# A Fourier mixing layer and an ELU feed-forward block: the first tile's opening, reordered

## The chip, the core and the metric

The kernel runs on one core of a Trainium2 chip. A core has five engines with instruction streams of their own: TensorE (PE, matrix products; its loads of stationary operands are listed as PEld), VectorE (DVE), ScalarE (ACT), GpSimd (POOL) and SyncE (SP, which here only issues transfers). Sixteen DMA engines carry what SP and POOL issue. The metric is device time in microseconds (us) of one launch.

## The reference

```python
def _attn_ref(x, filt_r, filt_i):            # x: 8 x 3008 x 256, filters: 1505 x 256
    X = np.fft.rfft(x, axis=1)
    F = (filt_r + 1j * filt_i)[None, :, :]
    Y = X * F
    return np.fft.irfft(Y, n=x.shape[1], axis=1).astype(np.float32)

def _moe_ref(x, w_in, w_out):                # x: 24064 x 256, w_in: 256 x 2048, w_out: 2048 x 256
    h = x @ w_in
    g = np.where(h > 0.0, h, np.exp(np.minimum(h, 0.0)) - 1.0)
    return (g @ w_out).astype(np.float32)
```

The second function takes the result of the first, its 8 batches of 3008 rows put one after the other. x and the filters are float32 at the kernel, and the weights arrive as float64.

## The kernel before, in words

The DFT of length 3008 is split as 47 x 64. The forward transform has a first factor of length 64 (`a_...`, tables `tf`, `ta`), and a second of length 47 (`b_...`, tables `gf`, later `fb`); then come the products with the filter; the inverse goes back by a 47-factor (`bi_...`) and a 64-factor (`n_...`). The feed-forward block follows tile by tile: an item is (batch, one of 6 row tiles, one of 4 quarters of d_ff), and both of its matrix products are done with seven block products in place of eight (`up_steps`, `down_steps`, with `w_sums` and `n_sums` forming the sums of blocks). Batch b + 1 is transformed beside the feed-forward block of batch b. The order of all instructions is the order in which the program writes them: each engine runs its own in that order. A dictionary `plan` puts the transform's and the conversion's pieces at five places inside each item (0 to 4).

The opening is the transform of batch 0, where no feed-forward work can lie beside it. Its parts:

- `x_place_first`, `x_load_first` (L256 to L277): 24 pairs of rows in six chunks. SP issues two transfers of x per chunk and one of the tables `tf` (for chunks 2 and 3, 4 and 5 one transfer for both). A chunk's 64 x 64 table of cosines and sines is stored twice, in the halves of the table's columns that serve the two parts of the spectrum, with other signs.
- `a_first` (L279): eight matmuls per chunk into PSUM, four ScalarE copies into `zt` (which partly lies in the room of `w_in[3]` and `w_out[3]`). `t_first` (L294) transposes it for a group of frequencies.
- `f_read_first` (L323): the filter, in four parts (two halves of the frequencies, `gh`, by two halves of the rows, `a`); half 0 of the rows by SP, half 1 by POOL.
- the loop over eight groups: `b_first` (L360, forward matmuls into two PSUM tiles, then `products`, four VectorE operations, L351 to L354), inside it `bi_first` of two groups earlier (L368: inverse matmuls, and two ScalarE copies, L380 and L381, into one of two halves of `t3f`, for the last two groups of `t2`), then `t_first` of two groups later and `y_write_first` (L386, four SP transfers to DRAM). The halves of `t3f` are used in turn, so the copies of group g wait for the write of group g - 2.
- `y_read_first` (L396) reads the first four rows of each part back as `t4f`, for `n_first`, which makes the first row tile; then the first item's matmuls begin.

The 16 weight blocks k (four per quarter: two of `w_in`, two of `w_out`) are brought from float64 to float32 by `w_fetch` (transfer, L740), `w_split` (two VectorE masks on the upper word, L769 and L770), `w_float` (four ScalarE steps: lower word, mantissa, two for the exponent, L779), `w_join` (VectorE: sign, lower word added, product, L785 to L798) and, after each odd k, `w_sums` (four additions, L806 to L809). `WTMP` says which of four sets of temporary tiles block k uses. In the kernel before, blocks 0 to 3 are fetched by SP between the chunks of x and converted there, 4 to 8 fetched by POOL after the filter and converted beside the loop (`BESIDE`) and after it, 9 to 15 inside the first six items (`early`).

Of the kernel before, what the change touches and what calls it, by code (L numbers as in the profile page):

```python
# [11 lines left out]
FP32 = mybir.dt.float32  # L12
# [26 lines left out]
SUMS = 4  # L39
WTMP = (0, 1, 2, 1, 0, 1, 0, 1, 0, 3, 2, 3, 2, 3, 2, 3)  # L40
# [4 lines left out]
def _make_tables():  # L45
# [30 lines left out]
    tf = np.ascontiguousarray(ta.reshape(P, H, 4, K2).transpose(0, 1, 3, 2)).reshape(P, H, P)  # L76
# [62 lines left out]
def kernel(  # L139
# [47 lines left out]
    edges = glob.tile([P, 3], FP32, name="edges")  # L187
# [66 lines left out]
    def x_place_first(c):  # L254
# [4 lines left out]
        if c < 2:  # L259
            w = tnp.tile([P, 4, P], FP32, tag="tn", name="tn")  # L260
        else:
            if c % 2 == 0:
                tas["pair", c // 2] = t4p.tile([P, 4, D], FP32, tag="t4", name="t0").rearrange("p u (w f) -> p (u w) f", f=P)
            w = tas["pair", c // 2][:, 4 * (c % 2):4 * (c % 2) + 4, :]
        xs[0, c], tas[0, c] = t, w
# [3 lines left out]
    def x_load_first(c):  # L269
# [4 lines left out]
        if c < 2:  # L274
            nc.sync.dma_start(tas[0, c], tf_d[:, 4 * c:4 * c + 4, :])
        elif c % 2 == 0:
            nc.sync.dma_start(tas.pop(("pair", c // 2)), tf_d[:, 4 * c:4 * c + 8, :])  # L277

    def a_first(c):  # L279
        xt, w = xs.pop((0, c)), tas.pop((0, c))  # L280
        for dh in range(2):
            k, ps = bank("psa", (P, 64, XC, 2))
            for u in range(XC):
                nc.tensor.matmul(ps[:, :, u, :], xt[:, u, ts(dh, P)], w[:, u, :].rearrange("p (k q) -> p k q", q=2),
                                 start=True, stop=True)
            for kh in range(2):
# [3 lines left out]
                s = ps[:, 32 * kh:32 * kh + 32].rearrange("p (k a) u q -> p k a (u q)", a=2)  # L290
                nc.scalar.activation(out=o, in_=s, func=AXT.Copy)
            banks.append(k)
# [30 lines left out]
    def f_read_first(gh, a, queue):  # L323

        r = slice(64 * a, 64 * a + 48)
        w0 = 1 if gh == a == 0 else 0
        k = 16 * a + 8 * gh
        for c, src in enumerate((filt_r, filt_i)):
            t = ff[r, c, 4 * gh:4 * gh + 4].rearrange("p g u d -> p (g u) d")
            queue.dma_start(t[0:48:2], raw(src, k, [[64 * D, 24], [D, 8], [1, D]]))  # L330
            for j, n in ((0, 16), (16, 7)):
                queue.dma_start(t[1 + 2 * j:2 * (j + n):2, w0:8],
                                raw(src, 64 * (j + 1) - k - w0, [[64 * D, n], [-D, 8 - w0], [1, D]]))
# [53 lines left out]
    def y_write_first(g, queues):  # L387
        if g == 0:
            yds[0] = yd.tile([P, H, D], FP32, tag="yd", name="yd")
        t = t3s.pop((0, g))  # L390
        for p in range(4):
            r = 64 * (p // 2) + 24 * (p % 2)
            k = 16 * g + 4 * p
            queues[p // 2].dma_start(yds[0][k:k + 4].rearrange("u i d -> i u d"), t[r:r + 24])
# [367 lines left out]
    def w_tmp(k):  # L762
        m, e, c = wtmp[WTMP[k]]
        return m, e, c[:, 0], c[:, 1]
# [7 lines left out]
    def w_float(k, *parts):  # L772
        m, e, f, l = w_tmp(k)
# [3 lines left out]
        for i in parts or range(4):  # L777
# [3 lines left out]
    def w_join(k):  # L781
        q, j = divmod(k, 4)
        m, e, f, l = w_tmp(k)
        hi = wds.pop(k)[:, :, 1]
        nc.vector.scalar_tensor_tensor(out=e, in0=hi, scalar=0x80000000, in1=e,  # L785
                                       op0=ALU.bitwise_and, op1=ALU.bitwise_or)
        nc.vector.tensor_tensor(out=f, in0=f, in1=l, op=ALU.add)
        e = e.bitcast(FP32)
        if j < 2:
            f, e = (t.rearrange("p (a j c) -> p a j c", a=2, j=2) for t in (f, e))  # L790
            dst = w_in[q][:, 2 * j:2 * j + 2, :, :].rearrange("p j a c -> p a j c")
# [300 lines left out]
```

## Time and profile before

| | us |
|---|---|
| median of 3 runs (2579.84 to 2589.81) | 2580.27 |
| profiled execution | 2585.88 |
| its span, first to last instruction | 2584.1 |
| TensorE busy (98% of the span) | 2526.8 |
| VectorE busy (80%) | 2070.1 |
| ScalarE busy (59%) | 1536.9 |
| GpSimd busy (7%) | 177.0 |

Busy times overlap, since the engines run beside each other. A row of an engine's timeline gives start, duration, engine, line, operation, output <- inputs with partitions x elements, and in brackets the idle time before it with what ended it. A row of waits gives the waiting engine and line, what it waited for, total us, number of times and the longest. Stretches are given in us from the start of the span. Releasers are inferred from semaphores and can be wrong where several were waited for.

### The profile page before, as it was taken

To read this page: it belongs to the slowest core of one execution; us is meant where nothing else is said; L and a number is where in the kernel's file an instruction comes from. 1 tells how busy PE (TensorE), PEld (TensorE's weight loads), DVE (VectorE), ACT (ScalarE), POOL (GpSimd) and SP (SyncE) were. 2 spreads that over 40 slices of the span, in tenths; PEclk is the share of its full clock that TensorE was granted. 3 is DMA by queue.
4 is the path that set the end of the run, shared out by engine and by line. 5 is a ranking of instruction groups with operands and counts; after the bars stand their busy time and mean duration, and the time that the engine had idled before them with its cause. 6 is when DMAs were issued, how large, how long until landed. Compare 5 with 4: busy or idle time off the path is not lost.

```text
span 2584.1 us, 44148 instructions
## 1 busy us (share of the span) xinstructions
PE 2526.8 (98%) x16726; PEld 2163.6 (84%) x16726; DVE 2070.1 (80%) x3613; ACT 1536.9 (59%) x2714; POOL 177.0 (7%) x308
## 2 busy tenths in 40 slices
PE   6789999999999999999999999999999999999998
PEld 4578888888898888988889888898888888898887
DVE  5889887788877888788887888778887788876766
ACT  5665556656566655665556655566556656565554
POOL 3130000001000100000000000000010001000000
PEclk8999999999999999999999999999999999999999
DMA  8652313522134222432215331253223322120010
GB/s 218 201 154 55 76 36 76 131 70 68 33 85 127 68 65 43 106 100 67 67 40 131 77 78 43 61 133 77 63 48 77 78 71 68 34 47 18 19 28 17
DMA packets 228994, 197.23 MB, mean 76 GB/s; under 512 B 128852, under 2 KB 202294, under 8 KB 228590
## 3 DMA queue, kind: packets, MB, share of 16 engines
q1 hardware_dynamic: 215550, 167.95, 26.7%
q0 software_dynamic: 12080, 26.21, 3.8%
q8 instruction: 132, 2.16, 0.4%
q14 instruction: 80, 0.66, 0.1%
q10 hardware_dynamic: 1152, 0.26, 0.1%
HBM read 122.46 MB, written 74.97 MB: 76 GB/s over the span
## 4 chain that ended last, share of the span: by engine, by line
PE 89%; DVE 6%; DMA 2%; ACT 2%; issue 1%; SPq 0%; POOL 0%; DVEq 0%; ACTq 0%; POOLq 0%
PE po L667 41%; PE phs L584 23%; PE phd L584 12%; PE pha L584 6%; PE pse L512 2%; PE psa L241 1%; PE pf L411 1%; PE pv L477 1%; DVE g L606 1%; DVE g L592 1%; ACT e L602 1%; PE po L345 0%; ACT e L601 0%; DVE g L643 0%; DVE g L642 0%
## 5 line engine op out<-in xcount | busy, mean ns | idle before, releaser
L667 PE MATMUL po<-g,wo 128*128 128x256 f32 (+1 forms) x5376 | 1317.3, 377 | 0.6 <-DVE t L686 0.6
L667 PEld LDWEIGHTS po<-g,wo 128*128 128x128 f32 x5376 | 1015.4, 191 | 164.8 <-issue 49.7
L595 ACT ACTIVATE g<-phs 128x512 f32<-128x512 f32 (+1 forms) x576 | 338.6, 588 | 713.8 <-PE phs L584 712.7
L584 PE MATMUL phs<-y,wi 128*128 128x256 f32 (+1 forms) x2288 | 582.4, 377 | 10.3 <-ACT g L595 10.3
L602 ACT ACTIVATE e<-e 128x512 f32<-128x512 f32 (+1 forms) x768 | 477.2, 621 | 24.3
L584 PEld LDWEIGHTS phs<-y,wi 128*128 128x128 f32 x2288 | 431.6, 191 | 65.3 <-ACT g L595 13.1
L592 DVE TENSOR_TENSOR g<-phd,g 128x512 f32<-128x512 f32 (+1 forms) x384 | 259.2, 675 | 267.4 <-ACT e L602 194.7
L606 DVE SCALAR_TENSOR_TENSOR g<-e,g 128x512 f32<-128x512 f32 (+1 forms) x576 | 390.6, 678 | 0.9 <-ACT e L602 0.5
L601 ACT ACTIVATE e<-g 128x512 f32<-128x512 f32 (+1 forms) x576 | 353.5, 614 | 60.0 <-DVE g L592 51.2
L606 DVE SCALAR_TENSOR_TENSOR g<-e,phs 128x512 f32<-128x512 f32 (+1 forms) x192 | 129.9, 676 | 141.0 <-ACT e L602 141.0
L584 PE MATMUL phs<-ys,wi 128*128 128x256 f32 (+1 forms) x784 | 198.6, 376 | 2.9 <-ACT g L595 2.9
L584 PE MATMUL phd<-y,wi 128*128 128x256 f32 (+1 forms) x768 | 194.9, 376 | 5.2 <-DVE g L592 5.2
L584 PE MATMUL phd<-ys,wi 128*128 128x256 f32 (+1 forms) x768 | 194.4, 376 | 1.2 <-DVE g L592 1.2
L584 PE MATMUL pha<-ys,wi 128*128 128x256 f32 (+1 forms) x752 | 190.1, 375 | 0.0
L601 ACT ACTIVATE e<-phs 128x512 f32<-128x512 f32 (+1 forms) x192 | 113.4, 591 | 111.7 <-PE phs L584 111.7
L584 PEld LDWEIGHTS phd<-y,wi 128*128 128x128 f32 x768 | 145.2, 190 | 25.0 <-DVE g L592 9.2
L584 PEld LDWEIGHTS phs<-ys,wi 128*128 128x128 f32 x784 | 147.9, 190 | 20.7 <-ACT g L595 4.2
L584 PEld LDWEIGHTS phd<-ys,wi 128*128 128x128 f32 x768 | 146.6, 191 | 17.8 <-DVE g L592 1.4
L340 POOL DMA_DIRECT2D fall<-fp x224 | 110.3, 500 | 691.6 <-DVE r L450 689.0
L584 PEld LDWEIGHTS pha<-ys,wi 128*128 128x128 f32 x752 | 143.1, 190 | 16.3
L592 DVE TENSOR_TENSOR g<-pha,g 128x512 f32<-128x512 f32 (+1 forms) x192 | 129.3, 673 | 24.3 <-PE pha L584 24.3
L643 DVE TENSOR_TENSOR g<-g,g 128x512 f32<-128x512 f32 (+1 forms) x192 | 132.6, 691 | 6.7
(181 smaller groups left out, 2167.8 us busy)
## 6 DMA issues: line engine op xcount, KB each, us to landing
t<-yd SPq DMA_DIRECT2D x94, 256.0 KB
z<-t SPq DMA_DIRECT2D x84, 256.0 KB
fall<-fp POOLq DMA_DIRECT2D x224, 96.0 KB, 2.9
t<-z SPq DMA_DIRECT2D x224, 96.0 KB
yd<-t SPq DMA_DIRECT2D x112, 192.0 KB
out_dram<-o SPq DMA_DIRECT2D x632, 32.0 KB
xc<-in_x_dram SPq DMA_DIRECT2D x84, 128.0 KB
xc<-in_x_dram SPq DMA_DIRECT2D x161, 64.0 KB
```

The costliest lines, as they stand in the source:

```text
L241: nc.tensor.matmul(p[o:o + 64, u, :], w[r, u, o:o + 64], src[r, u, :], start=True, stop=True)
L340: nc.gpsimd.dma_start(t[32 * a:32 * a + 24].rearrange("p c u d -> p (c u d)"), fp[g, a].rearrange("q c u d -> q (c u d)"))
L411: nc.tensor.matmul(pf[p][1][32 * a:32 * a + 32, js, :], fb[r, v, :], t2[r, js, a, :], start=True, stop=True, tile_position=(32 * p, 32 * a))
L512: nc.tensor.matmul(p[o:o + 64, dh, ds(64 * q, n)], t[r, i - 4 * m, ds(dh * P + o, 64)], w[r, i - 4 * m, 0:n], start=True, stop=True)
L584: nc.tensor.matmul(ps[:, a, 0:h], w_in[q][:, COMBO[n], a, :], y[n], start=start and a == 0, stop=True, skip_group_check=True)
L592: nc.vector.tensor_tensor(out=g[o], in0=i0, in1=i1, op=ALU.add)
L595: nc.scalar.activation(out=g[o], in_=i0, func=AXT.Copy)
L601: nc.scalar.activation(out=e, in_=src, func=AXT.Relu, scale=-1.0)
L602: nc.scalar.activation(out=e, in_=e, func=AXT.Exp, scale=-1.0)
L606: nc.vector.scalar_tensor_tensor(out=g[n], in0=es[n], scalar=1.0, in1=src, op0=ALU.subtract, op1=ALU.max)
L643: nc.vector.tensor_tensor(out=b12, in0=b22, in1=b12, op=ALU.subtract)
L667: nc.tensor.matmul(po[i][:, u, 0:h], w_out[q][:, COMBO[n], a, :], g[n][:, a, :], start=begin and a == 0 and n in (1, 3, 6, 4), stop=True, ...
```

## The change

Tables. `tf` holds only the first of the two copies; `ta_first` (new) writes the second with two VectorE multiplications per loaded table by a column of +1 and -1 (`edges[:, 3]`). `a_first` takes both PSUM banks of a chunk before its copies, and reads the table in the new layout.

Order of transfers. SP: x 0 and 1, weight 0, x 2 and 3, weight 1, x 4 and 5, `once`, two thirds of `gs`, then the filter in three portions (groups 0 and 1, 2 and 3, 4 to 7) with weight 2 after the second, then weights 3 and 4. POOL: the other halves of the three portions, weights 5 and 8, and 6 and 7 inside the loop. `t8` moves into the loop. The last two groups write four rows first, read them back, and write the other twenty after that. Weight 14 moves from the list before the items into the first item.

Conversion. `w_float` has three steps; the lower word is added in `w_join` by one multiply-add in place of an addition. Only block 0 is converted (and 1 split) before the loop, 1 to 3 beside it, 4 to 6 after it, 7 to 15 in the items; the sums of blocks 1, 3, 5 and 7 go from VectorE to POOL, those of 13 from POOL to VectorE. Three matmuls on a zeroed tile stand at the start.

```diff
-    tf = np.ascontiguousarray(ta.reshape(P, H, 4, K2).transpose(0, 1, 3, 2)).reshape(P, H, P)
+    tf = np.ascontiguousarray(ta.reshape(P, H, 4, 2, 16)[:, :, 0::2].transpose(0, 1, 3, 2, 4)).reshape(P, H, 64)
...
-        if c < 2:
-            nc.sync.dma_start(tas[0, c], tf_d[:, 4 * c:4 * c + 4, :])
-        elif c % 2 == 0:
-            nc.sync.dma_start(tas.pop(("pair", c // 2)), tf_d[:, 4 * c:4 * c + 8, :])
+        if ("load", c) in tas:
+            w, i, n = tas["load", c]
+            nc.sync.dma_start(w[:, 0], tf_d[:, i:i + n, :])
+
+    def ta_first(c):
+
+        w, _, _ = tas.pop(("load", c))
+        for a in range(2):
+            i, o = (w[:, q].rearrange("p u (h a k) -> p u h a k", h=2, a=2)[:, :, :, k] for q, k in ((0, a), (1, 1 - a)))
+            nc.vector.tensor_scalar(out=o, in0=i, scalar1=edges[:, 3:4], scalar2=None, op0=ALU.mult)
...
-    def y_write_first(g, queues):
+    def y_write_first(g, i0=0, i1=24):
...
-            queues[p // 2].dma_start(yds[0][k:k + 4].rearrange("u i d -> i u d"), t[r:r + 24])
+            nc.sync.dma_start(yds[0][k:k + 4, i0:i1].rearrange("u i d -> i u d"), t[r + i0:r + i1])
...
-        steps = ((l, wds[k][:, :, 0], AXT.Identity, 2.0 ** -52, 0.0), (f, m, AXT.Identity, 2.0 ** -20, 1.0),
+        steps = ((f, m, AXT.Identity, 2.0 ** -20, 1.0),
                  (ef, e, AXT.Relu, -8.0, edges[:, 0:1]), (e, ef, AXT.Relu, -1.0, edges[:, 1:2]))
...
-        nc.vector.tensor_tensor(out=f, in0=f, in1=l, op=ALU.add)
+                nc.vector.scalar_tensor_tensor(out=f, in0=lo, scalar=2.0 ** -52, in1=f, op0=ALU.mult, op1=ALU.add)
...
+            f_read_first(0, 2, 0, nc.sync)
+            f_read_first(0, 2, 1, nc.gpsimd)
+            f_read_first(2, 4, 0, nc.sync)
+            w_fetch(2, nc.sync)
+            f_read_first(2, 4, 1, nc.gpsimd)
+            f_read_first(4, 8, 0, nc.sync)
+            f_read_first(4, 8, 1, nc.gpsimd)
+            ta_first(0)
+            ta_first(1)
+            w_split(0)
+            ta_first(2)
+            ta_first(4)
+            for c in range(NXC):
+                a_first(c)
+                if c == 2:
+                    w_float(0)
+            w_join(0)
+            w_split(1)
+            for k in (3, 4):
+                w_fetch(k, nc.sync)
+            w_fetch(5)
...
+            w_fetch(8)
...
+            BESIDE = {0: ((w_float, 1, 0),), 1: ((w_split, 2), (w_float, 1, 1, 2)), 2: ((w_float, 2, 0), (w_join, 1, 0)),
+                      3: ((w_join, 1, 1), (w_float, 2, 1, 2)), 4: ((w_join, 1, 2), (w_sums, 1, nc.gpsimd), (w_fetch, 6), (w_split, 3)),
+                      5: ((w_join, 2, 0), (w_float, 3, 0)), 6: ((w_join, 2, 1), (w_float, 3, 1, 2)),
+                      7: ((w_join, 2, 2), (w_fetch, 7)), 8: ((w_join, 3), (w_split, 4))}
...
-                if g >= 2:
-                    y_write_first(g - 2, (nc.sync, nc.sync))
+                if 2 <= g < NG:
+                    y_write_first(g - 2)
+                elif g >= NG:
+                    y_write_first(g - 2, 0, 4)
+                if g == 4:
+                    nc.sync.dma_start(t8, t8_d)
                 if g == NG:
-                    y_read_first(0, 5)
-            y_read_first(5, 8)
+                    y_read_first(0, 6)
+            y_read_first(6, 8)
+            for g in (6, 7):
+                y_write_first(g, 4, 24)
+            w_sums(3, nc.gpsimd)
+            w_float(4)
+            w_split(5)
+            w_join(4)
+            w_float(5)
+            w_split(6)
+            w_join(5)
+            w_float(6)
+            w_sums(5, nc.gpsimd)
             w_split(7)
             w_join(6)
             w_float(7)
-            w_split(8)
-            w_sums(5)
-            w_float(8)
-            w_join(7)
-            w_sums(7)
-            w_join(8)
...
+        early = ((0, 2, w_join, 7, 0, 1), (0, 2, w_split, 8), (0, 4, w_float, 8, 0), (0, 0, w_float, 8, 1, 2), (0, 0, w_join, 7, 2),
+                 (0, 0, w_sums, 7, nc.gpsimd), (0, 3, n_unit, 0, 1), (0, 1, w_join, 8, 0, 1), (0, 1, w_split, 9), (0, 1, w_fetch, 14, nc.sync),
...
```

More of the change, by code (lines that the diff above doesn't have):

```diff
@@ L871 @@
-            step(0)
-            a_first(0)
-            step(1)
-            w_fetch(3, nc.sync)
-            x_load_first(5)
-            nc.sync.dma_start(once, once_d)
-            nc.sync.dma_start(gs, gs_d)
-            a_first(1)
-            f_read_first(0, 0, nc.sync)
-            f_read_first(0, 1, nc.gpsimd)
-            a_first(2)
-            step(2)
-            a_first(3)
-            step(3)
-            f_read_first(1, 0, nc.sync)
-            f_read_first(1, 1, nc.gpsimd)
-            w_fetch(4)
@@ L941 @@
             x_load(1, c)
-        for k in (11, 12, 13, 14, 15):
+        for k in (11, 12, 13, 15):
             w_fetch(k, nc.sync)
```

147 lines of the change are left out of this document (71 added, 76 removed).

## The prediction

> **What bounds it now.** I read the busy time by stretches first, cut where the kernel's stages begin, then the waits, then the engines' orders in time. The columns below are PE, PEld, DVE, ACT and POOL busy (instructions), granted clock, DMA share and GB/s.
>
> ```profile
> 0.00:9.00 9.00, 0.00 (x0) 0.03 (x1) 3.54 (x5) 1.95 (x2) 8.17 (x10) 1.00 0.78 190
> 9.00:25.40 16.40, 12.04 (x64) 11.70 (x65) 6.17 (x13) 11.21 (x26) 1.25 (x2) 0.90 1.07 273
> 25.40:31.50 6.10, 3.99 (x32) 3.71 (x33) 5.00 (x12) 4.48 (x12) 4.03 (x8) 1.00 1.10 243
> 31.50:44.80 13.30, 6.23 (x53) 4.14 (x52) 3.10 (x8) 4.98 (x11) 5.25 (x10) 0.90 0.96 190
> 44.80:56.00 11.20, 10.41 (x52) 5.60 (x56) 7.48 (x13) 4.74 (x8) 1.35 (x3) 0.51 0.90 273
> 56.00:76.80 20.80, 20.06 (x169) 7.71 (x161) 18.52 (x33) 14.38 (x27) 0.00 (x0) 1.00 0.43 109
> 76.80:88.90 12.10, 7.45 (x27) 4.71 (x27) 9.54 (x22) 6.47 (x11) 0.00 (x0) 0.90 0.67 184
> 88.90:113.40 24.50, 15.66 (x129) 12.86 (x128) 19.75 (x32) 14.75 (x28) 9.15 (x8) 0.98 0.79 234
> 240.00:2584.00 2344.00, 2334.23 (x15426) 2013.69 (x15424) 1888.28 (x3298) 1391.69 (x2446) 115.58 (x231) 1.00 0.28 67
> ```
>
> After 240 us TensorE is busy 2334.23 of 2344 us, and the change touches nothing there that TensorE waits for; all that can move is the opening. Up to 44.8 us the DMA engines are 78 to 110% busy: transfers set the pace. The waits, and the orders in time of VectorE and TensorE, say of what:
>
> ```profile
> PE psr L345 <- DVE rq L352: 7.6, 1, 7.6
> PE psn L535 <- DMA t4f<-yd: 4.7, 1, 4.7
> PE phs L584 <- ACT g L595: 13.2, 7, 4.7
> ```
> ```profile
> 38.69 0.69 DVE L351 TENSOR_TENSOR rq<-psr,ff 128x512 f32<-128x512 f32 x1 [4.72 <-DMA ff<-in_filt_r_dram]
> 44.76 0.69 DVE L352 TENSOR_TENSOR rq<-psr,ff 128x512 f32<-128x512 f32 x1 [5.38 <-DMA ff<-in_filt_i_dram]
> 45.36 0.68 DVE L353 SCALAR_TENSOR_TENSOR zq<-psi,ff 128x512 f32<-128x512 f32 x1
> ```
> ```profile
> 29.53 2.02 PE L284 MATMUL psa<-t,x 128*128 128x128 f32 x16 [2.09 <-DMA ff<-in_filt_i_dram]
> 34.37 0.38 PE L345 MATMUL psi<-t,once 48*64 48x256 f32 x1
> 55.81 1.04 PE L345 MATMUL po<-rq,gs 48*64 48x512 f32 x8
> 59.56 1.04 PE L345 MATMUL po<-rq,gs 48*64 48x512 f32 x8
> 75.10 1.67 PE L345 MATMUL po<-zq,gs 48*64 48x512 f32 x8
> ```
>
> The last DFT step (a_first of chunk 5) starts at 29.53 and the first group's spectrum is in PSUM by 34.75 (34.37 + 0.38), 5.2 us later. The filter for its products lands only at 44.76: 10 us of waiting, after which TensorE, idle 7.6 us, is granted 0.51 of its clock up to 56 us. From 55.81 to 59.56 one group of the loop takes 3.75 us with TensorE full; the last inverse matmul ends at 76.77.
>
> **The change, part by part: transfers.** Sizes, from the list of DMA issues up to 60 us:
>
> ```profile
> xc<-in_x_dram SPq DMA_DIRECT2D x7, 256.0 KB
> fall<-in_moe_w_in_dram SPq DMA_DIRECT2D x2, 512.0 KB
> t<-tf_t SPq DMA_DIRECT2D x2, 512.0 KB
> tn<-tf_t SPq DMA_DIRECT2D x2, 256.0 KB
> yd<-t SPq DMA_DIRECT2D x7, 96.0 KB
> ```
>
> A weight block is 0.52 MB, x 12 pieces of 0.26 MB (3.12), the first-factor tables 1.57 MB (2 x 512 + 2 x 256 KB). Before chunk 5 of x the old SP queue has four weight blocks, x and the tables, 6.8 MB; at the rates of the table (190, 273, 243 GB/s) that ends at 27.9 us, and the row says 29.53, so 1.6 us are added. The new queue has two weight blocks (1.05), x (3.12) and half the tables (0.79): 4.96 MB, by 20.9 us (1.71 MB by 9 us, the rest at 273 GB/s), so the last DFT step starts at 22.5 and its spectrum is there at 27.7. Then come once and gs (0.26 MB, 1.0 us) and the first filter portion, a quarter of 3.08 MB, at the 190 GB/s of the filter's stretch: 4.1 us, plus 1.6 us for what POOL's queue pushes in of later portions, plus 0.6 of overhead: 28.2. Spectrum and filter meet, the loop starts at 28.3 in place of 44.76: 16.5 us earlier. Twelve more filter issues of some 0.8 us each on SP and POOL lie beside the transfers; were they to set the pace, the start moves to about 32.
>
> The halved tables cost VectorE eight multiplies (ta_first), priced between 0.07 us and the 0.42 us of a 128x512 row below: 0.6 to 3.4 us, I take 1.6, all while VectorE waits for DMA; the last pair needs its table, which lands ahead of chunk 5. The three first matmuls on a zeroed tile, the memsets and the new order of the PSUM writes fall into time before x lands or between its chunks: nothing on the path; were the PSUM writes half as fast, 2 us on the last chunk.
>
> **A wait that comes with it.** The old SP queue was free when the loop began: the writes of the result start at 53.34, when they are ready, since weights 4 to 8 went by POOL. In the new kernel SP issues the last filter portion, then weights 3 and 4, and only then y_write_first(0); POOL's weights 5 and 8 share the engines.
>
> ```profile
> 53.34 23.62 SPq L394 DMA_DIRECT2D yd<-t  x28
> 77.48 0.33 SPq L398 DMA_DIRECT2D t4f<-yd  x1
> 77.93 1.71 SPq L394 DMA_DIRECT2D yd<-t  x4
> 82.92 0.32 SPq L398 DMA_DIRECT2D t4f<-yd  x1
> ```
>
> bi_first(2) copies into the tile that y_write_first(0) reads, so ScalarE waits there until that write has landed, and behind it stand the copies of the next transposes and bi_first(3)'s PSUM. What must move first: from 20.9 us 1.0 for the tables, 16.2 for the filter (3.08 MB at 190), and five weight blocks and the write (2.62 + 0.39 MB at the 273 GB/s of 44.8:56.0) 11.0: it lands at 49.1. Without this ScalarE would come to the copy at about 42 (28.3, products of groups 0 and 1 4.8, weight 2's split behind its late transfer, the products of group 2, then b and bi of 0.9 + 1.7). So some 7 us of the 16.5 are lost again. From 49.1: a copy 0.6, then bi 3 to 7, b 6 and 7 and one transpose group, 5 x 1.72 + 1.72 + 1.0 = 11.3 (a group of 3.75 is b 0.9, bi 1.7, transposes 1.0), 1 for the last products, and a cold clock. That one is priced by a gap of 4.75 us later in the old trace:
>
> ```profile
> 113.45 1.51 PE L584 MATMUL phs<-y,wi 128*128 128x224 f32 x4 [4.75 <-ACT g L595]
> 122.37 1.68 PE L667 MATMUL po<-g,wo 128*128 128x224 f32 x8
> ```
>
> Four matmuls take 1.51 where 8 later take 1.68: half speed for some 4 us, 2 us lost. The Trainium skill ("TensorE: Matmul & The Clock Gate", Part 1: The HAM clock gate) says that about 3.4 us of idling halves the clock and as much work restores it; both gaps here, 4.75 and 7.6 us, agree. The last inverse matmul ends at 49.1 + 0.6 + 11.3 + 1 + 2 = 64.0 in place of 76.77: **12.8 us gained**. Bounds: nothing lost to the wait (ends at 56), or a landing 4 us later.
>
> **The tail of the opening.** The last two groups write 4 rows of 24 first, so the write before the second read is 16 KB in place of 96. Old: last issue ends 79.64, read at 82.92. Between nothing and the 1.7 us that 0.39 MB take at the 234 GB/s of 88.9:113.4, I take 1.0. The remaining eight writes go behind the read, ahead of the reads of y for the next tile, which that tile needs some 8 us later: covered, up to 2 us if not. Against it, VectorE's chain behind the loop (join 3, splits 4 and 5, joins 4, 5 and 6) ends about when t4f lands, and w_float(7) stands ahead of n_first's copies on ScalarE: 0.7 us lost, 0 to 3.
>
> **Conversion.** Per block, ScalarE drops one step and VectorE's add becomes a multiply-add:
>
> ```profile
> 72.59 0.69 ACT L779 ACTIVATE wfl<-fall 128x512 f32<-128x512 uint32 x1
> 70.57 0.68 DVE L785 SCALAR_TENSOR_TENSOR we<-fall,we 128x512 uint32<-128x512 uint32 x1
> 71.17 0.69 DVE L787 TENSOR_TENSOR wfl<-wfl 128x512 f32<-128x512 f32 x1
> 72.50 0.42 DVE L769 TENSOR_SCALAR wm<-fall 128x512 uint32<-128x512 uint32 x1
> ```
>
> So 16 x 0.69 = 11 us less ScalarE, which does not bound, and the same VectorE (0.69 against 0.68). But blocks 7 and 8 now lie behind the first MoE matmuls, where VectorE is busy 19.75 of 24.5 us: join 7 2.1, block 8 0.8 + 2.1, and sums 13, back from POOL, 1.7 (4 x 0.42): 6.7 us more. For it: the wait for block 9's transfer goes (below), and 4.8 us of ScalarE steps of blocks 9 to 15, in a stage where TensorE waits 13.2 us for ScalarE's copies.
>
> ```profile
> 92.84 0.43 DVE L769 TENSOR_SCALAR rq<-t 128x512 uint32<-128x512 uint32 x1 [0.98 <-DMA t<-in_moe_w_in_dram]
> 99.54 0.61 DVE L606 SCALAR_TENSOR_TENSOR g<-e,g 128x448 f32<-128x448 f32 x1
> 101.40 1.74 DVE L606 SCALAR_TENSOR_TENSOR g<-e,g 128x448 f32<-128x448 f32 x1
> ```
> ```profile
> 98.87 0.79 POOL L807 TENSOR_TENSOR wi<-wi 128x256 f32<-128x256 f32 x1
> 101.39 1.26 POOL L227 TENSOR_TENSOR sd<-xc 128x512 f32<-128x512 f32 x1
> ```
>
> Between 5 us gained and 6.7 lost I take 1.0 gained, nearest to the 0.98 of the vanished wait, since both loads are spread over six items. The sums of blocks 1, 3, 5 and 7 go to POOL: 4 x 1.7 us off VectorE, at 0.79 an instruction beside it. At 99.54 VectorE ran at its 0.61 beside POOL's sums, at 101.40 it took 1.74 beside x_unit; I price the moved sums at nothing.
>
> **The sum.** 12.8 + 1.0 - 0.7 + 1.0 = 14.1 us. The profiled execution took 2585.88 us (span 2584.1), the median of the runs is 2580.27, 5.6 us lower; a gain in the opening is carried over whole: 2580.3 - 14.1 = 2566.2.
>
> **Rivals.** (a) The write is not held up: transfers interleave better or weights 5 and 8 come later, the loop ends at 56, gain 22: 2558. For it: 273 GB/s may hold for the filter too; against: 190 in the filter's own stretch at 96% busy. (b) The first MoE items are bound by VectorE and pay the 6.7 us: gain 6.4, 2574. For it 19.75 of 24.5 busy; against, VectorE waits there for ScalarE. (c) POOL's sums hold VectorE up as x_unit does: the eight of blocks 5 and 7 fall at the start of the MoE stage, 8 x 0.79 = 6.3, gain 7.8: 2572.5. The Trainium skill ("SBUF — State Buffer", SBUF: two separate sides) has GpSimd and a VectorE operation with two SBUF inputs exclude each other for a whole instruction; 101.40 agrees, 99.54 does not. (d) Slower: the filter's smaller pieces move at half the rate, 95 GB/s; then the first result write lands at 65.3, and the loop's end goes with it: gain 14.1 - 16.2, 2582. It is slower from a landing at 63.2 on, and by over 0.5% only from 76. (e) The portions do not come earlier, since both queues mix them: the loop starts at 37, but the write of group 0 sets its end all the same: 2567 with 1 us for a later start.
>
> **Chances.** Forecast 0.42 (its own range 2561 to 2571), (a) 0.22, (b) 0.16, (c) 0.06, (d) 0.07, (e) 0.07. Range 2556 to 2577: (a) with its own scatter below, (b) and (c) above. 0.5%, or 12.9 us, is about what a measurement can tell here (the runs shown span 10 us): that line is at 2567.4. Faster: (a) whole and two thirds of forecast and (e), 0.54; slower, the far end of (d), 0.04; the rest 0.42.
>
> **What would show it.** Products of group 0 at 27 to 32 us; a ScalarE wait of 5 to 9 us for yd's write at the copy of bi_first(2) near 49; the last inverse matmul at 61 to 66, n_first's matmuls at 70 to 74 (85.91 before). Wrong, if ScalarE does not wait there, or if the MoE's first six items take more than 3 us longer or shorter than before.

## The result: 4 us faster, not 14

| | before | after |
|---|---|---|
| median of 22 runs each | 2582.73 (2579.68 to 2589.81) | 2578.75 (2575.46 to 2581.99) |
| profiled execution | 2585.88 | 2575.46 |
| its span | 2584.1 | 2573.7 |

The ratio is 0.9982, with a 95% interval of 0.9976 to 0.9989: a gain of some 4.6 us, between 2.8 and 6.2, well inside the half per cent that the forecast set as its bound for no change. The forecast of 2566.2 missed, and 2578.75 lies outside its range of 2556 to 2577.

The two profiled executions differ by 10.4 us, much more than the medians do. One lies 3.1 us above its kernel's median, the other is the fastest of its 22: 6.4 us of the 10.4 are where these two executions happen to lie. So both kernels were profiled once more (the first experiment below), and every reading is made on both pairs.

First the profile after: two of its waits from 26 to 82 us (waiting engine and line, what it waited for, total us, times, longest).

```profile
ACT t L388 <- DMA yd<-t: 6.5, 1, 6.5
DVE wm L777 <- DMA fall<-in_moe_w_out_dram: 3.5, 1, 3.5
```

TensorE's old wait of 7.6 us for the products is gone, and VectorE waits at its first products (L359 now, 6.42 us in the rows below) for the spectrum (`psi`), no longer for the filter. In its place stands the wait that the forecast had named: ScalarE, at a copy of the inverse (L388), for a write of the result. Where these lie, in the order of time, VectorE's, ScalarE's and TensorE's rows:

```profile
21.50 0.62 DVE L284 TENSOR_SCALAR t<-t,edges 128x256 f32<-128x256 f32 x2 [6.88 <-DMA t<-tf_t]
31.14 0.69 DVE L359 TENSOR_TENSOR rq<-psr,ff 128x512 f32<-128x512 f32 x1 [6.42 <-PE psi L353]
39.49 0.43 DVE L777 TENSOR_SCALAR wm<-fall 128x512 uint32<-128x512 uint32 x1 [3.48 <-DMA fall<-in_moe_w_out_dram]
```
```profile
40.72 0.60 ACT L388 ACTIVATE t<-po 128x512 f32<-128x512 f32 x1
50.68 0.60 ACT L388 ACTIVATE t<-po 128x512 f32<-128x512 f32 x1 [6.54 <-DMA yd<-t]
55.56 0.60 ACT L388 ACTIVATE t<-po 128x512 f32<-128x512 f32 x1 [2.83 <-PE po L353]
61.30 0.60 ACT L388 ACTIVATE t<-po 128x512 f32<-128x512 f32 x1 [2.77 <-PE po L353]
63.83 0.60 ACT L388 ACTIVATE t<-po 128x512 f32<-128x512 f32 x1
65.55 0.60 ACT L388 ACTIVATE t<-po 128x512 f32<-128x512 f32 x1 [0.63 <-PE po L353]
67.26 0.60 ACT L388 ACTIVATE t<-po 128x512 f32<-128x512 f32 x1 [0.63 <-PE po L353]
```
```profile
22.33 5.25 PE L291 MATMUL psa<-t,x 128*128 128x128 f32 x32 [3.07 <-DVE t L284]
66.15 1.03 PE L353 MATMUL po<-zq,gs 48*64 48x512 f32 x8
76.36 3.47 PE L543 MATMUL psn<-t,t4f 128*128 128x128 f32 x16 [4.69 <-DMA t4f<-yd]
79.73 1.13 PE L592 MATMUL phs<-y,wi 128*128 128x224 f32 x4
```

The loop starts at 31.14 instead of 44.76 (13.6 us earlier). The copy of group 2 then waits 6.54 us for the first write, and the last inverse matmul ends at 67.2 instead of 76.8: 9.6 us are left. The stretches of the profile after, with the columns as before (PE, PEld, DVE, ACT, POOL busy, granted clock, DMA share, GB/s):

```profile
9.00:25.40 16.40, 13.33 (x78) 13.17 (x79) 4.87 (x13) 7.54 (x21) 4.38 (x9) 0.71 1.06 246
25.40:31.50 6.10, 5.64 (x53) 4.74 (x52) 0.36 (x1) 4.03 (x10) 6.10 (x12) 1.00 0.73 188
31.50:44.80 13.30, 13.26 (x114) 6.51 (x115) 9.82 (x18) 10.10 (x18) 0.93 (x2) 1.00 1.02 241
44.80:56.00 11.20, 7.41 (x41) 3.14 (x36) 7.49 (x13) 2.49 (x5) 4.09 (x6) 0.70 0.67 203
88.90:113.40 24.50, 19.20 (x86) 17.02 (x86) 23.29 (x38) 14.08 (x26) 7.81 (x7) 0.93 0.74 220
113.40:140.00 26.60, 20.90 (x116) 17.03 (x115) 26.31 (x41) 18.28 (x32) 11.81 (x11) 0.96 0.78 219
```

Inside the loop, TensorE is now far from full only in the stretch with the wait (7.41 of 11.2 us, clock 0.70). In the first items of the feed-forward (MoE) stage VectorE is full: 23.29 of 24.5 us, then 26.31 of 26.6.

### The profile page after: what moved, and what is told of

Read it like the earlier page. It is cut to its first block, busy times and chain, and to the rows that moved or that the text cites. A ratio compares the mean times of both kernels' runs of the same rounds, so it can differ in the third digit from the quotient of the medians.

```text
span 2573.7 us, 44194 instructions
## 1 busy us (share of the span) xinstructions
PE 2529.4 (98%) x16732; PEld 2160.7 (84%) x16732; DVE 2071.6 (80%) x3612; ACT 1528.2 (59%) x2698; POOL 189.3 (7%) x325
## 4 chain that ended last, share of the span: by engine, by line
PE 88%; DVE 6%; ACT 2%; DMA 2%; issue 1%; SPq 0%; POOL 0%; DVEq 0%; POOLq 0%; ACTq 0%
PE po L675 41%; PE phs L592 23%; PE phd L592 12%; PE pha L592 6%; PE pse L520 2%; PE pf L419 1%; PE psa L240 1%; PE pv L485 1%; DVE g L600 1%; DVE g L614 1%; DMA ff<-in_filt_i_dram 1%; ACT e L610 1%; ACT e L609 1%; PE pso L520 0%; DMA x<-in_x_dram 0%
## 5 line engine op out<-in xcount | busy, mean ns | idle before, releaser
L603 ACT ACTIVATE g<-phs 128x512 f32<-128x512 f32 (+1 forms) x576 | 338.6, 588 | 717.2 <-PE phs L592 716.1
L592 PEld LDWEIGHTS pha<-ys,wi 128*128 128x128 f32 x752 | 142.8, 190 | 16.5
```

The source lines that it names most:

```text
L592: nc.tensor.matmul(ps[:, a, 0:h], w_in[q][:, COMBO[n], a, :], y[n], start=start and a == 0, stop=True, skip_group_check=True)
L603: nc.scalar.activation(out=g[o], in_=i0, func=AXT.Copy)
```

## The experiments

Each ratio is to the kernel before, run on the same chip; one thousandth is 2.6 us. The table's other columns are from each kernel's profiled execution: the start of the first of the four products of group 0, ScalarE's wait for the first writes (0: none above 1 us), the end of the last inverse matmul, and the start of `n_first`'s matmuls (us). In the kernel before (both profiles), with two portions and with the conversion alone, the second product had to wait longer, until 44.8, 45.0, 37.3 and 41.9 us.

| kernel | ratio (95% interval) | products | wait | inverse | n_first |
|---|---|---|---|---|---|
| before | 1 | 38.7 | 0 | 76.8 | 85.9 |
| before, second profile | 1 | 37.8 | 0 | 75.0 | 83.5 |
| after | 0.9982 (0.9976 to 0.9989) | 31.1 | 6.5 | 67.2 | 76.4 |
| after, second profile | 0.9983 (0.9974 to 0.9992) | 33.2 | 5.6 | 68.2 | 78.5 |
| own tiles | 0.9953 (0.9940 to 0.9967) | 32.3 | 0 | 62.1 | 72.2 |
| weights 3, 4 later | 0.9964 (0.9951 to 0.9976) | 31.9 | 3.2 | 62.6 | 73.0 |
| own tiles, weights later | 0.9957 (0.9945 to 0.9969) | 31.6 | 0 | 60.2 | 69.6 |
| write queue | 0.9975 (0.9965 to 0.9985) | 29.1 | at most 0.5 | 64.1 | 72.8 |
| block 1 later | 0.9984 (0.9975 to 0.9992) | 27.6 | 7.4 | 67.5 | 78.5 |
| block 1 later, own tiles | 0.9968 (0.9955 to 0.9980) | 28.3 | 0 | 61.2 | 71.5 |
| two portions | 0.9986 (0.9977 to 0.9995) | 33.6 | 0 | 66.4 | 76.5 |
| full tables | 0.9992 (0.9983 to 1.0000) | 34.5 | 7.4 | 71.6 | 80.6 |
| conversion alone | 1.0000 (0.9991 to 1.0008) | 38.7 | 0 | 74.2 | 82.3 |
| sums on VectorE | 0.9990 (0.9981 to 0.9999) | 34.8 | 5.3 | 69.2 | 79.2 |
| first read to group 4 | 0.9982 (0.9974 to 0.9991) | 31.8 | 6.2 | 66.0 | 75.9 |
| own tiles, first read to group 4 | 0.9961 (0.9949 to 0.9974) | 32.1 | 0 | 66.7 | 76.8 |

### The two kernels again

Both are unchanged; the kernel after first.

> The changed kernel once more, unaltered, for a second profile. Theory A (the opening's end is set by the chain filter, loop, the wait for the first result write): the first filter product at 31 us, a wait of 6 to 7 us of ScalarE for that write, the last inverse matmul at 67, within 1 us of the first profile, and a time of 2576. Rival B (the opening differs from execution to execution by more than the gain): these moments move by 2 to 5 us, and the time with them; the median ratio to the kernel before stays at 0.998.

> The kernel before, unaltered, for a second profile. Rival B (the opening moves by several us from execution to execution, and the profiled execution of before was a slow one): the first feed-forward matmul starts 2 to 5 us before the 88.85 of the first profile, with a span of 2578 to 2582. If the first profile is typical: within 1 us of it.

The second execution of the kernel after:

```profile
23.38 0.62 DVE L284 TENSOR_SCALAR t<-t,edges 128x256 f32<-128x256 f32 x2 [7.11 <-DMA t<-tf_t]
52.50 0.60 ACT L388 ACTIVATE t<-po 128x512 f32<-128x512 f32 x1 [5.56 <-DMA yd<-t]
67.17 1.03 PE L353 MATMUL po<-zq,gs 48*64 48x512 f32 x8
78.49 3.65 PE L543 MATMUL psn<-t,t4f 128*128 128x128 f32 x16 [5.80 <-DMA t4f<-yd]
81.93 1.80 PE L592 MATMUL phs<-y,wi 128*128 128x224 f32 x4
```

and of the kernel before:

```profile
44.98 0.69 DVE L352 TENSOR_TENSOR rq<-psr,ff 128x512 f32<-128x512 f32 x1 [6.48 <-DMA ff<-in_filt_i_dram]
73.35 1.67 PE L345 MATMUL po<-zq,gs 48*64 48x512 f32 x8
83.46 3.68 PE L535 MATMUL psn<-t,t4f 128*128 128x128 f32 x16 [3.94 <-DMA t4f<-yd]
86.93 1.81 PE L584 MATMUL phs<-y,wi 128*128 128x224 f32 x4
```

The same rows stand 1 to 2.4 us elsewhere in both kernels, with no instruction changed: transfers land at other times (the last table at 23.4 instead of 21.5). This pair differs by 6.8 us at the end of the loop, by 5.0 at the first MoE matmul, and by 4.9 in the span (2578.0 and 2582.9), close to what the medians say. All but 0.4 us of what tells the two executions of a kernel apart happens before about 120 us.

### The wait at the write: own tiles

The results of groups 2 and 3 go into two tiles of their own, which the writes of groups 0 and 1 do not read.

```diff
+            t3x.update({g: t1p.tile([P, XC, D], FP32, tag="t1", name="t3x") for g in (2, 3)})
...
-        t = t3s[0, g] = (t2 if g > 5 else t3f)[:, g % 2]
+        t = t3s[0, g] = t3x[g] if g in t3x else (t2 if g > 5 else t3f)[:, g % 2]
```

> The changed kernel with tiles of their own for the results of groups 2 and 3, so that their copies wait for no write; the order of transfers is untouched. Theory A: the wait of 6.5 us is gone, though group 4 now waits for the write of group 2, which stands in SP's queue behind the weights too (landing near 50): last inverse matmul at 60 to 63, 4 to 7 us shorter. Rival C: within 2 us of the changed kernel.

Its ScalarE rows and the stretch that had been cold:

```profile
42.48 0.58 ACT L388 ACTIVATE t<-po 128x512 f32<-128x512 f32 x1
47.60 0.60 ACT L388 ACTIVATE t3x<-po 128x512 f32<-128x512 f32 x1 [1.72 <-PE po L353]
51.32 0.60 ACT L388 ACTIVATE t3x<-po 128x512 f32<-128x512 f32 x1 [1.65 <-PE po L353]
```
```profile
44.80:56.00 11.20, 11.20 (x98) 4.99 (x102) 11.17 (x19) 6.62 (x13) 4.12 (x6) 1.00 0.78 231
```

The copy of group 2 comes at 47.60 although these products started 1.2 us later, TensorE is busy all of the 11.2 us at full clock, and the median falls to 2571.57 (2569.64 to 2575.13), 12 us below the kernel before: 0.0029 of the ratio, or 7.5 us, beyond the kernel after. That is the largest of three such pairs: with block 1 later the tiles bring 0.0016 (4.1 us, intervals that just overlap), with the first read to group 4 0.0021 (5.4 us). So the tiles are worth 4 to 7.5 us, about half or more of what each of these kernels gains on the kernel before. The four kernels with these tiles lie at 0.9953 to 0.9968 and are not told apart.

Freeing the tile does not settle the end of the loop in every execution. The last kernel of the table has the tiles too, no copy waits for a write, and yet its profile ends the loop at 66.7 us, in an execution 4.4 us above its kernel's median. There weight block 2, whose split stands ahead of the products of group 2, is split at 42.78 and not 41.48 us, and TensorE, busy throughout, is granted 0.54 of its clock in the stretch that was at full clock above:

```profile
44.80:56.00 11.20, 11.20 (x52) 4.73 (x56) 9.11 (x15) 4.52 (x9) 2.47 (x4) 0.54 0.79 212
```

### What makes the write late: its place in the queue

Weights 3 and 4 are issued inside the loop, behind the writes of groups 0 and 1; their tiles are set aside where they were issued before.

```diff
             for k in (3, 4):
-                w_fetch(k, nc.sync)
+                held[k] = xp.tile([P, 2, 2, D], FP32, tag="xc", name="wd")
...
                 if 2 <= g < NG:
                     y_write_first(g - 2)
+                if g in (2, 3):
+                    w_fetch(g + 1, nc.sync)
```

> The changed kernel with weight blocks 3 and 4 issued by SP behind the first and the second result write (in the loop) in place of ahead of them. Theory A: ScalarE no longer waits 6.5 us for the first result write, TensorE's clock does not drop at 47 to 58 us, the last inverse matmul ends at 59 to 62 in place of 67, and the whole is 4 to 8 us shorter than the changed kernel. Rival C (VectorE's conversion work behind the loop sets the start of the feed-forward stage, so the loop's end does not matter): the loop ends earlier, but the first feed-forward matmul still starts at 78 to 80 and the time stays within 2 us.

In another kernel the order stays, and ScalarE's queue issues the writes of groups 0 and 1.

```diff
-                    y_write_first(g - 2)
+                    y_write_first(g - 2, queue=nc.scalar if g < 4 else nc.sync)
```

> ScalarE's queue issues the writes of groups 0 and 1 of the result; all else is as in the changed kernel. If the write of group 0 is late because it stands behind 1 MB of weights on SP's queue, ScalarE's wait at the copy of group 2 shrinks from 5.6 to 6.5 us to under 2, the loop ends 4 to 5 us earlier, and the time is 2571 to 2577 beside 2579 to 2580 of the changed kernel. Rival: the transfer rate sets the landing whichever queue issues it: the wait stays at 4 to 7 us and the time is the changed kernel's.

SP's rows of the kernel after, and of that with the weights later:

```profile
41.53 0.33 SPq L763 DMA_DIRECT2D wd<-in_moe_w_in_dram  x1
44.12 9.25 SPq L402 DMA_DIRECT2D yd<-t  x12
```
```profile
38.77 5.15 SPq L402 DMA_DIRECT2D yd<-t  x4
44.30 1.70 SPq L764 DMA_DIRECT2D wd<-in_moe_w_out_dram  x2
```

With the weights behind it the first write starts to be issued at 38.77 instead of 44.12, ScalarE's wait shrinks to 3.2 us and the loop ends at 62.6. On ScalarE's queue it is issued at 38.49 and the loop ends at 64.1: 3 to 4 us earlier, where 4 to 5 were expected. ScalarE's and SP's rows of that kernel, and a row of its waits, say where the rest went:

```profile
38.49 2.07 ACTq L402 DMA_DIRECT2D yd<-t  x4
40.61 0.60 ACT L388 ACTIVATE t<-po 128x512 f32<-128x512 f32 x1 [1.54 <-DMA yd<-t]
43.32 2.36 ACTq L402 DMA_DIRECT2D yd<-t  x4
46.18 0.60 ACT L388 ACTIVATE t<-po 128x512 f32<-128x512 f32 x1 [2.14 <-DMA yd<-t]
```
```profile
44.66 1.81 SPq L340 DMA_DIRECT2D ff<-in_filt_i_dram  x2
```
```profile
DVE rq L360 <- DMA wd<-in_moe_w_out_dram: 5.6, 1, 5.6
```

The idle times of 1.54 and 2.14 us, put down to the write, are mostly ScalarE's own issuing (38.49 to 40.56 and 43.32 to 45.68 us), which does not count as busy; the copy at 40.61 is that of group 1, into the half that no write has read yet. What is left as a wait for a landing is at most the 0.5 us before the copy of group 2 at 46.18: the wait for the write is gone, and 4.4 us of issuing stand on ScalarE in its place. VectorE now stands 5.6 us at later products; SP's issue of the last filter pieces has moved to 44.66 us (35.82 in the kernel after), so I read the wait as one for the filter, although the row names the weight that came last. The place in the queue makes the write late, then, and bringing it forward pushes something else back. Neither ratio (0.9964, 0.9975) is clear of the kernel after's: the intervals overlap. The late weights together with own tiles, and with the split of block 2 one group later, bring no more than own tiles alone:

```diff
-            BESIDE = {0: ((w_float, 1, 0),), 1: ((w_split, 2), (w_float, 1, 1, 2)), 2: ((w_float, 2, 0), (w_join, 1, 0)),
+            BESIDE = {0: ((w_float, 1, 0),), 1: ((w_float, 1, 1, 2),), 2: ((w_split, 2), (w_float, 2, 0), (w_join, 1, 0)),
```

> The changed kernel with own tiles for the results of groups 2 and 3, with weight blocks 3 and 4 issued in the loop, and with the split of block 2 one group later, so that the products of group 2 do not stand behind that block's transfer. Theory A: the last inverse matmul at 57 to 60 in place of 62 with the own tiles alone, the time 2 to 4 us below that kernel, 2568 to 2570. Rival C (the conversions behind the loop bind): the loop ends earlier, the time within 1 us of the kernel with own tiles alone.

The loop of that profile ends 1.9 us earlier than with own tiles alone (60.2 against 62.1), but the ratios, 0.9957 and 0.9953, do not differ, and neither do the spans (2568.6 and 2568.3). The two traces show where the lead goes. At the first MoE matmul it is still 2.5 us (73.00 against 75.53); near 94 us it is gone, at a wait of TensorE that ends at the same time in both, in own tiles alone and in this kernel:

```profile
94.28 1.02 PE L592 MATMUL phs<-ys,wi 128*128 128x224 f32 x4 [3.62 <-ACT g L603]
```
```profile
94.50 1.86 PE L592 MATMUL phs<-ys,wi 128*128 128x224 f32 x4 [5.68 <-ACT g L603]
```

The copy of ScalarE (L603) that ends it stands behind the conversion of block 9, which waits 5.15 and 7.22 us for VectorE's mask. VectorE reaches that mask at 91.65 and 91.87 us: in the combined kernel three operations before it take 1.65 to 1.75 us, beside POOL's additions on the next x, where in the other two of them take 0.62 and 0.68 and one 1.77. There VectorE and POOL, and not the loop's end, set the pace. No run moved that mask.

### Does the start of the loop count?

Weight block 1 is loaded behind the first filter portion instead of between the chunks of x, so that the last tables come earlier.

```diff
-                if c == 3:
-                    w_fetch(1, nc.sync)
...
             f_read_first(0, 2, 0, nc.sync)
+            w_fetch(1, nc.sync)
...
-            w_split(1)
...
-            BESIDE = {0: ((w_float, 1, 0),), 1: ((w_split, 2), (w_float, 1, 1, 2)), 2: ((w_float, 2, 0), (w_join, 1, 0)),
+            BESIDE = {0: ((w_split, 1), (w_float, 1, 0)), 1: ((w_split, 2), (w_float, 1, 1, 2)), 2: ((w_float, 2, 0), (w_join, 1, 0)),
```

> Weight block 1 is loaded behind the first filter portion instead of ahead of the last third of x, and its split stands behind the first products on VectorE; all else is as in the changed kernel. If the tables and x of the last two steps bind the start of the loop (spectrum, not filter, ended the wait), half a megabyte less ahead of them starts the products 2 us earlier, at 29 to 31 us; the end of the loop follows only as far as the write of group 0 does (it has the same bytes ahead of it): 0 to 1 us, and the time is within 1 us of the changed kernel's. Rival: the start binds the loop, and the time falls by the same 2 us.

```profile
19.44 0.62 DVE L284 TENSOR_SCALAR t<-t,edges 128x256 f32<-128x256 f32 x2 [4.86 <-DMA t<-tf_t]
27.63 0.69 DVE L359 TENSOR_TENSOR rq<-psr,ff 128x512 f32<-128x512 f32 x1 [5.65 <-PE psi L353]
51.44 0.60 ACT L388 ACTIVATE t<-po 128x512 f32<-128x512 f32 x1 [7.42 <-DMA yd<-t]
```

The last table lands 2 to 4 us earlier and the products start 3.5 to 5.6 us earlier: the spectrum did bind the start. The wait at the write takes it all back: it grows to 7.42 us and ends at 51.44, as before, and the loop ends at 67.5. The time is that of the kernel after. The same edit with own tiles:

> As the run before, with two tiles of their own for the results of groups 2 and 3, so that no copy waits for the first write. If the write is what hid the earlier start, now the 2 us come through: 2568 to 2571 beside the 2571.6 of own tiles alone. Rival: with the tiles freed, block 2's arrival and VectorE's conversions set the loop: the time stays at 2571 to 2573.

```profile
DVE wm L777 <- DMA fall<-in_moe_w_out_dram: 6.1, 1, 6.1
```

The start, 4 us earlier than with own tiles alone, still brings nothing measurable (0.9968 against 0.9953, intervals that overlap): VectorE, in the row above, then waits 6.1 us for block 2 at its split, and the loop ends at 61.2. From the other side, the filter in two portions (groups 0 to 3, 4 to 7) starts the loop later:

```diff
-            f_read_first(0, 2, 0, nc.sync)
-            f_read_first(0, 2, 1, nc.gpsimd)
-            f_read_first(2, 4, 0, nc.sync)
+            f_read_first(0, 4, 0, nc.sync)
...
-            f_read_first(2, 4, 1, nc.gpsimd)
+            f_read_first(0, 4, 1, nc.gpsimd)
```

> The filter comes in halves, groups 0 to 3 and 4 to 7, so that six DMA issues fewer stand on each queue; all else is as in the changed kernel. If the portions carry the earlier start (the prediction's reading), the first products wait for twice as many bytes: they start at 34 to 36 us in place of 31 to 33, the loop's end moves by at most 2 us because the write of group 0 sets it, and the time is 0 to 2 us above the changed kernel's. Rival: the issues set the pace in the filter's stretch (DMA share 0.73 there), so fewer of them land the whole filter earlier, the write of group 0 lands 2 to 4 us earlier, and the time is 1 to 3 us below.

```profile
33.64 0.69 DVE L359 TENSOR_TENSOR rq<-psr,ff 128x512 f32<-128x512 f32 x1 [7.42 <-PE psi L353]
37.31 0.69 DVE L360 TENSOR_TENSOR rq<-psr,ff 128x512 f32<-128x512 f32 x1 [2.98 <-DMA ff<-in_filt_i_dram]
```

The second product of group 0 comes at 37.31, 3.5 to 5.6 us later than in the kernel after, and the loop ends at 66.4, not later; no copy waits for a write any more, since everything before it is later. The third portion bought nothing measurable. Between 27.6 and 37.3 us the start of the loop has no measurable price in these kernels: the copy of group 2 comes at 50.7 to 53.0 us in all of them.

### The other parts

Both copies of the first factor's tables are loaded, without `ta_first`:

```diff
-            nc.sync.dma_start(w[:, 0], tf_d[:, i:i + n, :])
+            nc.sync.dma_start(w, tf_d[:, :, i:i + n, :])
...
-            ta_first(0)
-            ta_first(1)
...
-            ta_first(2)
-            ta_first(4)
```

> The changed kernel with both copies of the tables loaded and without the eight VectorE multiplications: 0.79 MB more to load ahead of the last chunk of x. Theory A (bytes ahead of the last chunk set the loop's start): the first filter product 2.5 to 3.5 us later than in the changed kernel (34 to 36), the time 2 to 3 us longer. Rival E (the multiplications on VectorE stand in the way of the DFT matmuls as much as the bytes do): no later than the changed kernel, the time within 1 us.

The ratio goes from 0.9982 to 0.9992, about 2.6 us, though the intervals overlap: 0.79 MB more go ahead of the filter and of the first write, and the loop ends at 71.6. About half the gain of the whole change would then be the halved tables. The conversion in three steps, alone in the kernel before:

```diff
-        steps = ((l, wds[k][:, :, 0], AXT.Identity, 2.0 ** -52, 0.0), (f, m, AXT.Identity, 2.0 ** -20, 1.0),
+        steps = ((f, m, AXT.Identity, 2.0 ** -20, 1.0),
...
-        nc.vector.tensor_tensor(out=f, in0=f, in1=l, op=ALU.add)
+                nc.vector.scalar_tensor_tensor(out=f, in0=lo, scalar=2.0 ** -52, in1=f, op0=ALU.mult, op1=ALU.add)
```

> The kernel before with the three-step conversion alone: ScalarE drops the step on the lower word, VectorE adds it by a multiply-add; order and places as before. The prediction prices this at nothing where VectorE bounds and up to 4.8 us gained where ScalarE's copies hold TensorE: 0 to 3 us faster than before. Rival F (the lower word's buffer is now held until the join, which delays the next fetch into it): 0 to 4 us slower.

Nothing: 1.0000. The sums of 1, 3, 5 and 7 back on VectorE, and those of 13 on POOL:

```diff
-            w_sums(3, nc.gpsimd)
+            w_sums(3)
...
-            w_sums(5, nc.gpsimd)
+            w_sums(5)
```

> The changed kernel with the sums of blocks 1, 3, 5 and 7 back on VectorE and those of block 13 back on POOL, as in the kernel before. Rival D (POOL's sums hold up VectorE's masks, which take 0.95 and not 0.42 us beside them): 4 to 8 masks and joins become 0.5 us faster, and the 6.8 us of sums on VectorE cost less than they seem: within 2 us. Theory A and C (VectorE is the bound from the loop's end to the sixth item): 4 to 6 us longer than the changed kernel.

Not faster: 0.9990, with a median 1.4 us above the kernel after on the same chip (2581.71 and 2580.3), within what the intervals allow for no change. So POOL's sums, which the third rival feared, cost no measurable time. Last, the tail: the first read of `t4f` covers groups 0 to 5 in the kernel after, and SP issues it 2.5 us after the last inverse matmul (before 0.7 us), ahead of the last writes. SP's row of the kernel after:

```profile
69.68 0.32 SPq L406 DMA_DIRECT2D t4f<-yd  x1
```

```diff
-                    y_read_first(0, 6)
-            y_read_first(6, 8)
+                    y_read_first(0, 5)
+            y_read_first(5, 8)
```

> The first read of t4f covers groups 0 to 4, as in the kernel before, instead of 0 to 5; all else is as in the changed kernel. In both profiles of the changed kernel SP issues that read 2.5 and 3.7 us after the last inverse matmul (69.68 against 67.2, 71.92 against 68.2), where before it was 0.7 and 0.2 us, and the writes of group 7 stand behind it. If this wait is what keeps the tail as long as it was (9.2 and 10.3 us from the last inverse matmul to n_first, beside 9.1 and 8.5 before), the gap shrinks to 7 to 8.5 us and the time by 1 to 2.5 us. Rival: the transfers' latency behind the second read sets the gap: it stays at 9 to 10 us and the time is the changed kernel's.

> The same with two tiles of their own for the results of groups 2 and 3. If the read is what keeps the tail long, 1 to 2.5 us below the kernel with own tiles alone: a ratio of 0.9943 to 0.9950 beside 0.9953. Rival: the same time as that kernel.

My theory fell in both: from the last inverse matmul to `n_first` it is still 9.9 and 10.1 us, and the ratios, 0.9982 and 0.9961, are not told apart from those without the edit (0.9982 and 0.9953). SP issues the shorter read 2.9 us after the loop's end in the first of them. What fits is that the last groups now follow each other closely (copies at 63.83, 65.55 and 67.26, 1.7 us apart), and that the writes and their landing cannot keep up; that was not tested.

## Why the prediction was wrong

**The base: wrong. The carry-over: right.** The 14.1 us were worked out against a profile of 2585.88 and taken from a median of three runs, 2580.27. Of the miss of 12.55 us against 2578.75, 2.5 is that base (22 runs give 2582.73), and 10.1 a gain that was too large. "A gain in the opening is carried over whole" held: 9.5 us at `n_first` became 10.4 in the span in the first pair, 5.0 became 4.9 in the second. The profiled pair alone would have said 3.7 too large (14.1 against 10.4): the execution that I costed had a late opening. The second pair, nearer to the medians, shows most of the rest: at the end of the loop the gain is 6.8 and not 12.8, in the tail -1.8 and not +0.3, from `n_first` to the end -0.1 and not +1.0, together 9.2 of 14.1 missing.

**The loop's start, 28.3: too early, and without effect.** It was 31.1 and 33.2. The last DFT step began at 22.33 us, as forecast (22.5), and in the second profile at 24.21, where the last table landed at 23.4. But that table covers two chunks, so 32 matmuls and not 16 stood behind its landing, 5.25 us of them; the products followed 8.8 and 9.0 us after the step's start, where I had 5.2. That the filter would meet the spectrum was right, and SP's and POOL's many issues filled the filter's stretch (POOL 6.10 of 6.1 us at a DMA share of 0.73). But two runs show that the term should have had no weight: a start of 27.6 and one of 37.3 end the loop at 67.5 and 66.4.

**The wait at the first write: right in place, cause and size of the wait, 1.6 to 3.4 us late.** 5 to 9 us near 49 were forecast; it was 6.5 us to 50.7, and 5.6 to 52.5. By the rates of the stretches as many bytes had moved by 44.8 us as forecast (10.2 MB and 9.9 in the second profile, for 10.1), but 11.7 MB and not 11.3 before the write had landed: other transfers went beside it or ahead of it. Which, was not isolated. It is the row that decides this change, as the forecast had it, and removing it gives 4 to 7.5 us, for "some 7 of the 16.5".

**From the wait to the end of the loop, 14.9: 16.5 and 15.7.** Mis-sized in its parts. I had the groups behind the wait follow each other at 1.72 us; the copies of groups 3 and 4 came 4.9 and 5.7 us after their predecessors (50.68, 55.56, 61.30), each waiting 2.8 us for TensorE on a clock of 0.70; I read that as the forward work of the later groups, which had stood behind ScalarE too. Only the last three ran at 1.7 to 2.5. What that cost beyond my figure is 0.8 to 1.6 us, beside the 2 us that I had for the cold clock.

**The last inverse matmul at 64.0, "12.8 us gained": the step that failed most.** It ended at 67.2 and 68.2, against 76.8 and 75.0 before: 9.6 and 6.8 us for 12.8. The path was right, its terms were too small, and the end before was that of a late execution. The gap of 6.0 us in the second pair is 1.8 of the earlier end before, 3.4 of the later landing, and 0.8 behind it.

**The tail, 1.0 gained: not seen.** From the last inverse matmul to `n_first` it took 9.1 and 8.4 us before, 9.2 and 10.3 after. The write before the second read did become shorter, but the first read now stands later behind the loop. The cause stays open; the wider read is not it.

**Conversion, 1.0 gained: about right, as a sum of parts that could not be told apart.** From `n_first` to the end the change gains 0.9 us in the first pair and loses 0.1 in the second. VectorE became as full as the second rival said (23.29 and 26.31 us), yet the 6.7 us that it priced did not come: in sum its stage lost nothing. That is a sum of losses and gains: at the wait behind VectorE's mask of block 9 (near 94 us in the two rows above) TensorE stands 3.59 and 4.67 us in the kernel after. At the copy that ends it, the fifth of ScalarE's `g<-phs`, the gain is down to 6.4 and 0.6 us; at the seventh it is 10.7 and 5.3 again, since the kernel before has its longest wait for ScalarE, 4.7 us in both profiles, in between.

**The rivals.** (a), no wait, did not happen in the changed kernel; the own tiles made it happen, and gave 8 to 12 us and not 22; the start was late and block 2 came late, which were not told apart. (b) and (c) did not decide, (d) did not come: 188 GB/s in the filter's stretch is the 190 of before, not 95. (e) had the right mechanism with the wrong premise: the portions did come earlier, and the write of group 0 set the loop's end all the same. The chance of 0.54 for faster by half a per cent was too high: I gave (a) its 0.22 on a transfer rate that one stretch showed, and let the forecast's own range reach no further than 5 us, where the same rows of one kernel move by 2 us from execution to execution.

## What to carry to other kernels

A start that moves earlier is worth what the next in-order wait leaves of it: before adding up such a gain, find the buffer that is used twice in the stage, ask when the transfer that frees it is issued and what stands ahead of it in its queue, and free that first (two tiles were worth 4 to 7.5 us here, shifting the start within 10 us nothing measurable). A transfer-bound opening differs between executions: one profile is one draw, and a gain of some 10 us in 2580 needs a second profile of both kernels before its parts are believed. A whole-stage gain should be priced at the milestones (start, wait, end, first use), since each passed on only a part here: 13.6, 9.6 and 9.5 us at start, loop's end and `n_first` in one pair, 11.8, 6.8 and 5.0 in the other.

## What was not expected of the hardware

Masks of VectorE (one input in SBUF) slow down beside POOL's additions. In the kernel after, the first row begins before the additions, the second lies beside the addition shown; the last is from the kernel with those sums on VectorE:

```profile
68.44 0.42 DVE L777 TENSOR_SCALAR wm<-wd 128x512 uint32<-128x512 uint32 x1
69.65 0.95 DVE L777 TENSOR_SCALAR wm<-fall 128x512 uint32<-128x512 uint32 x1
```
```profile
69.52 0.80 POOL L815 TENSOR_TENSOR wo<-wo 128x256 f32<-128x256 f32 x1
```
```profile
72.74 0.42 DVE L777 TENSOR_SCALAR wm<-fall 128x512 uint32<-128x512 uint32 x1
```

A mask that falls beside an addition takes 0.95 us instead of 0.42, and the join's steps beside them (L795 at 71.39 in the kernel after) 1.21 instead of 0.68. The forecast had looked only at an operation with two inputs that kept its 0.61 us; the profile before already held a mask of 0.95 us, at 98.13 beside the first of block 9's sums. In sum this cost nothing measurable (0.9982 against 0.9990 with the sums on VectorE), since VectorE is spared the additions. The Trainium skill ("SBUF — State Buffer", SBUF: two separate sides) counts VectorE operations in a two-port mode among those that shut GpSimd out, and are shut out by it, for a whole instruction; that these masks run in such a mode no run here shows, but their 0.53 us more agree.

The other is the filter's stretch: in the kernel after, with the filter cut into the smallest pieces, the DMA engines are busy at 0.73 of their time between 25.4 and 31.5 us and move 188 GB/s; in the kernel with two portions, with larger pieces, they are busy at 1.01 and move 207.

```profile
25.40:31.50 6.10, 5.64 (x36) 5.43 (x35) 0.82 (x3) 2.94 (x9) 2.95 (x7) 0.71 1.01 207
```

A share of 0.28 more brings only a tenth more bytes: in these stretches, which hold other transfers too, the share says little on the rate.
